# An attention and gated feed-forward kernel whose leftover rows are multiplied as block products of seven

## The chip, the core and the metric

The kernel runs on one core of a Trainium2 chip. The metric is the device time in microseconds (us), the median of several runs. Before the change it is 236.12 us (three runs, 235.85 to 236.62). The profiled execution spans 234.5 us from its first instruction to its last.

## What is computed

There are 8 batches of 8 heads with 576 tokens and 64 features each, and 32 memory slots. The heads of a token (8 x 64 = 512 features) go into a feed-forward block of width 1536.

```python
def _attn_ref(q, k, v, phi):
    a = exp(phi - phi.max(axis=2))         # axis 2: the tokens
    a = a / a.sum(axis=2)
    k_m = np.einsum('bhsm,bhsd->bhmd', a, k)
    v_m = np.einsum('bhsm,bhsd->bhmd', a, v)
    scores = (1 / sqrt(64)) * q @ k_m.T
    return softmax(scores) @ v_m

def _moe_ref(x, w_gate, w_val, w_out):
    g = x @ w_gate
    return silu(g) * (x @ w_val) @ w_out   # x: 4608 tokens x 512
```

(Cut, with softmax and silu written as names.)

## The kernel before

Batches 0 and 1 run together at the start. From batch 2 on, a batch has two parts. In the first, TensorE computes the attention scores, and between them the output products of the batch before. In the second, 24 slots of gate and value products run (`g`), each followed by a silu on ScalarE and a multiplication on VectorE; beside them the sums of the next batch's keys and values (`kv_items`) and the products of its values with the weights (rounds of u: `u_item`, `u_three`) are made, and copied from PSUM by ScalarE and VectorE.

The output product of a batch's first 512 tokens is a 2x2 block product made with seven products of half size instead of eight (`products`). Its sums of blocks, `t_S`, are made by `chunk_done` when a third of the hidden features is ready. Its seven results are combined in three PSUM banks, "homes" `s`, `a` and `c`:

```python
def products(b, by_hand):
    ...
    first = product("s", A(0, 0), W_(0, lo), "p1") + product("a", A(1, 0), W_(1, lo), "c11")
    five = product("c", Sx(0), T(0), "p5")
    six = product("s", Sx(1), T(1), "q6")
    three = product("c", Sx(3), W_(1, hi), "c12")
    seven = product("s", Sx(2), T(2), "c22")
    four = product("s", A(1, 1), T(3), "c21")
    if b + 1 == B:
        return first + six + five + seven + three + four, ops
    return first + five + six + three + seven + four, ops
```

Each `product` has six units of two matmuls with 256 columns. The last 64 tokens of each batch are left over. Two batches' leftovers make 128 rows (`xs[pair]`), which are multiplied plainly, in two column halves:

```python
def out_rest(pair, half):
    ...
    for jf in (2 * n, 2 * n + 1):          # unit n of 6
        nc.tensor.matmul(mine["p"], lhsT=xs[pair][:, jf]..., rhs=WO[jf][:, cols], ...)
    ...                                    # after the last unit: copy, and two stores
```

The main loop takes units from a backlog between other work. What a batch does in its first part, and which units go where:

```python
for b in range(2, B):
    last = b + 1 == B
    exp_tables()
    if b == 2:
        ...
        backlog = one[6:12] + zero[36:] + one[12:36]
        ops = ops1
    else:
        backlog += out_rest(b // 2 - 1, b % 2)
        run(take(6))
    if b > 2:
        loads(b)                           # the loads of batch b + 2
    for g in range(NG):
        scores(b, g)
    ...
    z_inv_v(b, 0)
    norm(b, 0)
    ops["c11"]()
    run(take(6))
    if not last:
        phi_exp(b + 1)
    z_inv_v(b, 1)
    norm(b, 1)
    run(take(6))
    run_late()
    nc.scalar.preload_act_table_set("silu_and_others")
    run(take(12))
    if b == 2:
        u_three(2)
        run(out_rest(0, 0))
        u_values(2)
        backlog = one[36:]
    g = gv_slots(b)
    beside = 0 if last else min(7, len(backlog))
    outs = [lambda: run(take(1)) for _ in range(len(backlog) - beside)]
    streams = [(g, 0, 24), (outs, 4, 24)]
    ...
    if not last:
        load_qT(b + 1)                     # queries transposed by a DMA of SyncE's queue
        if b > 2:
            phi_sum(b + 1)                 # GpSimd sums the phi weights, for kv_denominators
        else:
            streams += [([lambda: loads(2)], 7, 8)]
        streams += [
            (kv_items(b + 1, lambda: (u_item(b, 2, "aava")(), run(take(2)))), KV, KV + 4),
            ([lambda: (run(take(2)), u_three(b + 1), run(take(3)))], 19, 20),
        ]
    spread(*streams)
    flush_mul()
    units, ops = products(b, ("p1", "c11"))
    backlog += units
```

Numbers beside a stream are the slots between which its items are spread. The sums for the next batch begin with its denominators: nine narrow matmuls, or two where GpSimd has summed the weights before (`esums`):

```python
def run_sums():
    ...
    kv_denominators(b, p[0][:, o:o + NG])
    kv_sum(b, p, (0, 1))
    kv_reciprocal(b, p[0][:, o:o + NG])
    kv_norm(b, p)
    done(*p)
    if beside:
        beside()
```

At the end stand the last batch's products, and both halves of the last pair's leftovers; stores then alternate between the queues of SyncE and ScalarE.

Of the kernel before, what the change touches and what calls it, by code (L numbers as in the profile page):

```python
# [14 lines left out]
def kernel(  # L15
# [193 lines left out]
    def phi_sum(b):  # L209

        e = ephis[b].rearrange("p j i m -> p j (i m)")
        mark = att.tile([1, 1], BF16, tag="mark", bufs=1, name="t_mark")
        nc.gpsimd.tensor_copy(out=mark, in_=atts[b - 1, 1][0:1, 0, 0:1])  # L215
        t = att.tile([128, 4, 128], FP32, tag="es", bufs=1, name="t_es")
        add = lambda o, x, y: nc.gpsimd.tensor_tensor(out=o, in0=x, in1=y, op=ALU.add)  # L217
        add(t, e[:, 0:4], e[:, 4:8])
        add(t[:, 0:2], t[:, 0:2], t[:, 2:4])
        add(t[:, 0], t[:, 0], t[:, 1])  # L220
        add(t[:, 0], t[:, 0], e[:, 8])
        hl = att.tile([128, 2, 128], BF16, tag="ehl", bufs=1, name="t_ehl")
        nc.gpsimd.tensor_copy(out=hl[:, 0], in_=t[:, 0])
        nc.gpsimd.tensor_tensor(out=hl[:, 1], in0=t[:, 0], in1=hl[:, 0], op=ALU.subtract)
        esums[b] = hl
# [71 lines left out]
    def kv_items(b, beside=None):  # L297


        def run_sums():  # L300
            o = 2 * D
            p = [bank([128, CH], FP32, f"p_kv{g}") for g in range(NG)]
            kv_denominators(b, p[0][:, o:o + NG])
            kv_sum(b, p, (0, 1))
            kv_reciprocal(b, p[0][:, o:o + NG])
            kv_norm(b, p)
            done(*p)
            if beside:
                beside()

        return [run_sums, lambda: kv_T(b)]
# [273 lines left out]
    def chunk_done(b, c):  # L585
# [21 lines left out]
        end = c + 1 == NCH  # L607
        if (b, c) in ((0, 2), (1, 1), (1, 2)):
            late.append(lambda *part: sums(nc.gpsimd if b else nc.vector, *part))
        else:  # L610
            sums(nc.vector if end else nc.gpsimd)
        if end and b > 1:
            late.append(ends)
        else:
            ends()
        if (b, c) in beside_sums:
            beside_sums[b, c]()

# [4 lines left out]
    }  # L623

# [10 lines left out]
    def store(t_o, b, t0, count, row=0, cols=slice(0, 512), queues=None):  # L635

        if queues is None and box.get("end"):
            queues = nc.sync, nc.scalar
        for n, (r0, m, bb, jj, pp) in enumerate(token_segments(b, t0, count)):
            eng = queues[n % len(queues)] if queues else nc.sync  # L640
            eng.dma_start(out=out_r[bb, jj, pp:pp + m, cols], in_=t_o[row + r0:row + r0 + m])

    def out_rest(pair, half):

        h = DM // 2
        mine = {}
        cols = slice(h * half, h * half + h)

        def unit(n):
            def run():  # L650
                if n == 0:
                    mine["p"] = bank([128, h], FP32, "p_oo")
                for jf in (2 * n, 2 * n + 1):
                    nc.tensor.matmul(  # L654
                        mine["p"],
                        lhsT=xs[pair][:, jf].rearrange("p a t -> p (a t)"),
                        rhs=WO[jf][:, cols],
                        start=(jf == 0),
                        stop=(jf == NJF - 1),
                    )  # L660
                if n == NJF // 2 - 1:
                    t_o = work.tile([128, h], FP32, tag="to", name="t_o")
                    copy("v" if box.get("end") else "a", t_o, mine["p"])
                    done(mine["p"])
                    end = 2 * pair + 2 == B
                    for k in range(2):
                        store(
                            t_o, 2 * pair + k, S - 64, 64, 64 * k, cols,
                            ((nc.sync, nc.scalar)[k],) if end else None,
                        )  # L670

            return run

        return [unit(n) for n in range(NJF // 2)]

    def products(b, by_hand):
# [3 lines left out]
        lo, hi = slice(0, h), slice(h, DM)  # L680

        def A(e, n):
            return lambda c, m, u: hts[b, c][
                :, 2 * m + e, 256 * n + 128 * u:256 * n + 128 * u + 128
            ]

        def Sx(n):
            return lambda c, m, u: Ss[b, c][:, n, m, 128 * u:128 * u + 128]
# [7 lines left out]
        def product(home, lhs, rhs, after):  # L696
            def unit(k):
                c, m = k // 2, k % 2

                def run():  # L700
                    fresh = k == 0 and home not in mine
                    if fresh:
                        mine[home] = bank([128, 2, h], FP32, f"p_o{home}")
                        mine[home, "new"] = True
                    for u in range(2):
# [21 lines left out]
        def keep(name, home):  # L727
            def run():
                nc.scalar.copy(out=tile_of(name, tag=name, bufs=1), in_=mine[home])

            return run
# [6 lines left out]
        def both(name, t0, cols):  # L738
            for u in range(2):
                store(mine[name][:, u, cols], b, t0 + 128 * u, 128, cols=cols)  # L740

        def c11():
            t = tile_of("o1", (128, 2, DM), tag="to")
            add(t[:, :, lo], "a", "p1", True)
            if box.get("end"):
                both("o1", 0, lo)

        def c22():
            t = tile_of("o2", (128, 2, DM), tag="to")
            add(t[:, :, hi], "s", "p5")  # L750
            if box.get("end"):
                both("o2", 256, hi)

        def c12():
            t = mine["o1"]
            add(t[:, :, hi], "c", "q6", True)
            both("o1", 0, hi if box.get("end") else slice(0, DM))

        def c21():
            t = mine["o2"]  # L760
            copy("v" if box.get("end") else "a", t[:, :, lo], mine["s"])
            done(mine["s"])
            both("o2", 256, lo if box.get("end") else slice(0, DM))
# [4 lines left out]
        )  # L768
        now = {n: f for n, f in ops.items() if n not in by_hand}
# [6 lines left out]
        if b + 1 == B:  # L776
# [163 lines left out]
    def loads(b):  # L940

        if b + 2 < B:
            load_q(b + 2)
            load_phi(b + 2, nc.gpsimd)
            load_k(b + 2)
            load_v(b + 2)
# [7 lines left out]
    for b in range(2, B):  # L954
        last = b + 1 == B
        exp_tables()
        if b == 2:
            phi_exp(2)
# [14 lines left out]
            mark = att.tile([1, 1], BF16, tag="mark", bufs=1, name="t_mark")  # L973
            nc.gpsimd.tensor_copy(out=mark, in_=Ts[2][0:1, 3, 0, 0:1])
            for part in ((0, 1), (3,), (2,)):
                for c in (1, 2):
                    sums[1, c](part)
            backlog = one[6:12] + zero[36:] + one[12:36]
            ops = ops1
        else:  # L980
            backlog += out_rest(b // 2 - 1, b % 2)
            run(take(6))
        if b > 2:
            loads(b)
# [9 lines left out]
        norm(b, 0)  # L994
# [5 lines left out]
        norm(b, 1)  # L1000
        run(take(6))
        run_late()
        nc.scalar.preload_act_table_set("silu_and_others")
        run(take(12))
        if b == 2:
            u_three(2)
            run(out_rest(0, 0))
            u_values(2)
            backlog = one[36:]
        g = gv_slots(b)  # L1010
        beside = 0 if last else min(7, len(backlog))
        outs = [lambda: run(take(1)) for _ in range(len(backlog) - beside)]
        streams = [(g, 0, 24), (outs, 4, 24)]
        if last:
            streams += [([u_item(b, 2)], 5, 6)]
        if not last:
            load_qT(b + 1)
            if b > 2:
                phi_sum(b + 1)
            else:  # L1020
                streams += [([lambda: loads(2)], 7, 8)]
            streams += [
                (kv_items(b + 1, lambda: (u_item(b, 2, "aava")(), run(take(2)))), KV, KV + 4),
                ([lambda: (run(take(2)), u_three(b + 1), run(take(3)))], 19, 20),
# [8 lines left out]
    run(out_rest(B // 2 - 1, 0))  # L1033
    box["end"] = True
    run(take(6))
    ops["c11"]()
    run(backlog)
    run(out_rest(B // 2 - 1, 1))
# [28 lines left out]
```

The softmax here doesn't subtract the row's maximum and nothing guards it: scores larger than these inputs give would overflow.

## Time and profile before

| | before |
|---|---|
| median time | 236.12 us |
| span of the profiled execution | 234.5 us |
| TensorE busy | 225.9 us, 96% |
| VectorE busy | 187.4 us, 80% |
| ScalarE busy | 172.5 us, 74% |
| GpSimd busy | 135.2 us, 58% |
| granted TensorE clock | 1.000 |

In the profile, PE is TensorE, PEld its weight loads, DVE VectorE, ACT ScalarE, POOL GpSimd and SP SyncE; a "q" after a name is that engine's queue of transfers. "L706" is a line of the program: in the kernel before, L514 holds the gate and value products, L706 the main output products, L654 the leftovers' products, L471 the rounds of u, L235 and L263 the sums and denominators, L641 the stores. A busy share is time inside records of an instruction; matmul records overlap, so spacing between starts tells more of TensorE than the length of a record. The chain that ended last is followed back from the last instruction to what released it, step by step, and it shows which engine carried the time.

### The profile page before, as it was taken

The page shows a single profiled execution, that of the slowest core. Times are in us where ns is not written, and L with a number is a line of the kernel's source. Part 1 is how long each engine was busy: PE and PEld are TensorE (multiplying, and loading weights), DVE is VectorE, ACT ScalarE, POOL GpSimd, SP SyncE. Part 2 cuts the span into 40 slices and gives each one's busy share as a digit, 9 for nine tenths or more (in the row PEclk, how much of TensorE's full clock was granted, in tenths as well). Part 3 has the DMA queues.
Part 4 walks back from the last instruction along what each step waited for, and adds up shares of the span by engine and source line. Part 5 has one row for each costly group of instructions (what it writes and reads, how often), then busy time and mean ns, then how long its engine had stood idle before and what let it go on. Part 6 is the DMA issues. An engine that isn't in the chain of part 4 may idle for free.

```text
span 234.5 us, 7300 instructions
## 1 busy us (share of the span) xinstructions
PE 225.9 (96%) x2847; PEld 171.3 (73%) x2847; DVE 187.4 (80%) x417; ACT 172.5 (74%) x368; POOL 135.2 (58%) x171
## 2 busy tenths in 40 slices
PE   7998899999999999999999999999999999999992
PEld 2555466778887777887778777877788777878881
DVE  4157699999979697998799878988799879987621
ACT  2758888988447888977898779968897789677310
POOL 8532426999099159654992399267916493029400
PEclk9999999999999999999999999999999999999999
DMA  6999999999974999899559964999313721122134
GB/s 211 205 205 207 198 208 206 228 238 248 207 169 97 252 216 158 166 247 232 137 80 252 214 110 106 225 226 142 110 25 81 132 89 27 31 62 89 33 92 126
DMA packets 42914, 36.84 MB, mean 157 GB/s; under 512 B 15488, under 2 KB 38528, under 8 KB 42880
## 3 DMA queue, kind: packets, MB, share of 16 engines
q0 software_dynamic: 21440, 22.42, 55.0%
q1 hardware_dynamic: 20176, 12.79, 25.8%
q10 hardware_dynamic: 1264, 1.18, 1.6%
q8 instruction: 22, 0.36, 0.6%
q14 instruction: 12, 0.10, 0.1%
HBM read 42.47 MB, written 9.44 MB: 221 GB/s over the span
## 4 chain that ended last, share of the span: by engine, by line
PE 82%; DMA 8%; POOL 4%; DVE 3%; issue 1%; ACT 0%; DVEq 0%; POOLq 0%
PE p_g L514 20%; PE p_v L514 19%; PE p_os L706 16%; PE p_oc L706 8%; DMA t_kv<-in_v_dram 8%; PE p_u L471 5%; PE p_oo L654 5%; PE p_oa L706 4%; PE p_kv L235 2%; POOL t_es L217 1%; POOL t_q L108 1%; PE p_g L400 1%; POOL t_kv L98 1%; DVE t_lz L443 1%; DVE t_z L434 1%
## 5 line engine op out<-in xcount | busy, mean ns | idle before, releaser
L537 DVE TENSOR_TENSOR t_h<-t_sg,p_v 128x288 bf16<-128x288 bf16 x192 | 83.1, 452 | 15.6 <-PE p_v L514 7.6
L514 PEld LDWEIGHTS <-t_U 128*128 128x128 bf16 x768 | 73.7, 98 | 21.7 <-issue 2.9
L531 ACT ACTIVATE t_sg<-p_g 128x288 bf16<-128x288 f32 x192 | 74.5, 423 | 15.9 <-PE p_g L514 9.1
L514 PE MATMUL p_g<-t_A,t_U 128*128 128x288 bf16 x384 | 77.2, 286 | 0.0
L514 PE MATMUL p_v<-t_A,t_U 128*128 128x288 bf16 x384 | 77.0, 286 | 0.0
L706 PEld LDWEIGHTS <-t_S 128*128 128x128 bf16 x384 | 37.4, 98 | 4.5 <-issue 0.2
L601 POOL TENSOR_TENSOR t_S<-t_h 128x512 bf16<-128x512 bf16 x17 | 19.7, 1156 | 35.2 <-DVE t_h L537 35.2
L491 ACT CAST t_U<-p_u 128x512 bf16<-128x512 f32 x53 | 28.0, 608 | 8.9 <-PE p_u L471 8.9
L706 PEld LDWEIGHTS <-t_h 128*128 128x128 bf16 x288 | 27.3, 98 | 7.8 <-issue 4.0
L706 PE MATMUL p_os<-t_T,t_S 128*128 128x256 bf16 x192 | 23.7, 273 | 0.0
L559 POOL TENSOR_TENSOR t_S<-t_S,t_h 128x512 bf16<-128x512 bf16 x17 | 19.6, 1155 | 1.3
L559 POOL TENSOR_TENSOR t_S<-t_h,t_S 128x512 bf16<-128x512 bf16 x17 | 20.1, 1186 | 0.0
L559 POOL TENSOR_TENSOR t_S<-t_h 128x512 bf16<-128x512 bf16 x17 | 19.6, 1155 | 0.0
L471 PE MATMUL p_u<-W,t_kT 64*32 64x512 bf16 (+1 forms) x416 | 15.9, 363 | 0.1
L706 PE MATMUL p_os<-t_T,t_h 128*128 128x256 bf16 x96 | 15.6, 273 | 0.0
L827 PE MATMUL p_warm<-bones 128*128 128x512 bf16 (+2 forms) x43 | 12.9, 427 | 1.7 <-DVE bones L850 1.7
L451 DVE TENSOR_TENSOR t_A<-t_E,t_lz 128x576 bf16<-128x576 bf16 x16 | 13.4, 840 | 0.9 <-ACT t_lz L427 0.3
L654 PE MATMUL p_oo<-WO,t_x 128*128 128x256 bf16 x96 | 14.0, 273 | 0.0
L495 DVE CAST t_U<-p_u 128x512 bf16<-128x512 f32 x19 | 12.4, 683 | 1.6 <-PE p_u L471 1.6
L215 POOL COPY t_mark<-t_A 1x1 bf16<-1x1 bf16 x4 | 0.7, 182 | 20.3 <-DVE t_A L451 20.3
L706 PE MATMUL p_oc<-t_T,t_S 128*128 128x256 bf16 x96 | 12.0, 273 | 0.0
L706 PE MATMUL p_oa<-WO,t_h 128*128 128x256 bf16 x96 | 11.8, 273 | 0.0
(93 smaller groups left out, 309.9 us busy)
## 6 DMA issues: line engine op xcount, KB each, us to landing
t_kv<-in_k_dram POOLq DMA_DIRECT2D x8, 576.0 KB, 10.1
t_kv<-in_v_dram POOLq DMA_DIRECT2D x8, 576.0 KB, 14.4
out_dram<-t_o SPq DMA_DIRECT2D x21, 192.0 KB, 2.6
t_phi<-in_phi_dram POOLq DMA_DIRECT2D x6, 576.0 KB, 7.9
t_q<-in_q_dram POOLq DMA_DIRECT2D x5, 576.0 KB, 7.4
out_dram<-t_o SPq DMA_DIRECT2D x37, 64.0 KB, 2.0
out_dram<-t_o SPq DMA_DIRECT2D x14, 128.0 KB, 5.8
t_q<-in_q_dram POOLq DMA_DIRECT2D x6, 288.0 KB, 11.3
```

The costliest lines, as they stand in the source:

```text
L451: nc.vector.tensor_tensor(out=a, in0=es.pop((b, g)), in1=lzs.pop((b, g)), op=ALU.mult)
L471: nc.tensor.matmul(p[g][32 * i:32 * i + 32, o:o + n], lhsT=kTs[b][64 * g:64 * g + 64, 2, 32 * i:32 * i + 32], rhs=w_part(w, c, i, g, halve ...
L491: nc.scalar.copy(out=t, in_=p)
L495: nc.vector.tensor_copy(out=t, in_=p)
L514: nc.tensor.matmul(p[:, 0:HALF], lhsT=Us[b, c, g][:, o // 2, which, 128 * (o % 2):128 * (o % 2 + 1)], rhs=atts[b, g][:, r], start=(g == 0) ...
L531: nc.scalar.activation(out=sg, in_=gate[:, 0:HALF], func=AF.Silu)
L537: nc.vector.tensor_tensor(out=dst, in0=sg, in1=val[:, 0:HALF], op=ALU.mult)
L559: eng.tensor_tensor(out=out, in0=x, in1=y, op=ALU.subtract)
L601: eng.tensor_tensor(out=t[:, 0], in0=A21, in1=A22, op=ALU.add)
L654: nc.tensor.matmul(mine["p"], lhsT=xs[pair][:, jf].rearrange("p a t -> p (a t)"), rhs=WO[jf][:, cols], start=(jf == 0), stop=(jf == NJF - 1),)
L706: nc.tensor.matmul(mine[home][:, u], lhsT=lhs(c, m, u), rhs=rhs(c, m), start=fresh and u == 0, stop=(k == 5), skip_group_check=u == 1 or n ...
L827: nc.tensor.matmul(p[:, 0:128 * a], lhsT=bones, rhs=x.to_broadcast([128, a, 128]) if a > 1 else bones, start=True, stop=True,)
```

## The change

Four things are changed together.

1. Leftovers of four batches (256 rows, two pairs) are multiplied as one 2x2 block product with seven half-size products: one group in batch 4, one begun in batch 7 and finished at the end. GpSimd makes the four sums of blocks for each third of the hidden features (`quad_sums`). The plain products of leftovers go away.
2. The queries of batch 3 are transposed at the start of batch 2, and loads are issued at the end of a batch's second chunk, for the batch after the next but one.
3. GpSimd's work is set apart from VectorE's: two of the four sums of the second chunk wait until VectorE has done its sums of the third, norms are moved later, the phi weights' sums for batch 5 are left to TensorE, and where they are made, TensorE runs the big sums before the denominators.
4. At the end, the last batch's main stores all go through SyncE's queue, the last three leftover blocks' through two.

The core of the diff (cut where marked):

```diff
         def run_sums():
-            kv_denominators(b, p[0][:, o:o + NG])
+            behind = b in esums
+            if not behind:
+                kv_denominators(b, p[0][:, o:o + NG])
             kv_sum(b, p, (0, 1))
+            if behind:
+                beside()
+                kv_denominators(b, p[0][:, o:o + NG])
             kv_reciprocal(b, p[0][:, o:o + NG])
             kv_norm(b, p)
             done(*p)
-            if beside:
+            if beside and not behind:
                 beside()
...
+        fourth = b in (3, 7)
         if (b, c) in ((0, 2), (1, 1), (1, 2)):
             late.append(...)
+        elif b < 2:
+            sums(nc.gpsimd)
+        elif end:
+            sums(nc.vector)
+            if b + 1 == B:
+                second.pop()(nc.vector, (2, 3))
+                wait_for(Ss[b, 1][0:1, 3, 0, 0:1])
+            else:
+                wait_for(t[0:1, 3, 0, 0:1])
+                second.pop()(nc.gpsimd, (3, 2))
         else:
-            sums(nc.vector if end else nc.gpsimd)
-        if end and b > 1:
+            if c:
+                sums(nc.gpsimd, (0, 1))
+                second.append(sums)
+            else:
+                sums(nc.gpsimd)
+        if end and b > 1 and not fourth:
             late.append(ends)
         else:
             ends()
+        if b > 1 and c == 1:
+            loads(b + 3)
+        if b + 1 == B and end:
+            quad_sums(1)
...
+    def quad_sums(qd):          # x, y = the two pairs; A11, A12 of x, A21, A22 of y
+        for n in range(4):
+            for c in range(NCH):
+                if n == 0:
+                    nc.gpsimd.tensor_tensor(out=t[:, 0], in0=A21, in1=A22, op=ALU.add)
+                elif n == 1:
+                    subtract(nc.gpsimd, t[:, 1], t[:, 0], A11)
+                elif n == 2:
+                    subtract(nc.gpsimd, A21, A11, A21)
+                else:
+                    subtract(nc.gpsimd, t[:, 2], A12, t[:, 1])
...
-        if queues is None and box.get("end"):
-            queues = nc.sync, nc.scalar
-        for n, (r0, m, bb, jj, pp) in enumerate(token_segments(b, t0, count)):
-            eng = queues[n % len(queues)] if queues else nc.sync
+        for r0, m, bb, jj, pp in token_segments(b, t0, count):
+            eng = nc.sync
+            if queues:
+                turn[0] += 1
+                eng = queues[turn[0] % len(queues)]
...
-    def out_rest(pair, half):
-        ...
-    def products(b, by_hand):
+    def products(b, by_hand, quad=None):
+        U = 2 if quad is None else 1        # matmuls in a unit
...
+        def leftover(name, room, half, cols):
+            queues = (nc.sync, nc.scalar) if end and room else None
+            ...                             # add or copy out of PSUM, then two stores
...
         if b == 2:
+            load_qT(3)
...
-            backlog += out_rest(b // 2 - 1, b % 2)
             run(take(6))
-        if b > 2:
-            loads(b)
...
         z_inv_v(b, 0)
-        norm(b, 0)
...
         z_inv_v(b, 1)
-        norm(b, 1)
+        if b > 2:
+            norm(b, 0)
+            norm(b, 1)
         run(take(6))
         run_late()
+        if b == 4:
+            wait_for(atts[4, 1][0:1, 0, 0:1])
+            quad_sums(0)
-        run(take(12))
+        run(take(6))
         if b == 2:
+            norm(2, 0)
+        run(take(6))
+        if b == 2:
+            norm(2, 1)
             u_three(2)
-            run(out_rest(0, 0))
+            run(one[36:39])
             u_values(2)
-            backlog = one[36:]
+            backlog = one[39:]
         g = gv_slots(b)
+        quad = []
+        if b == 4:
+            quad = products(b, (), 0)[0]
+        if last:
+            rest, rest_ops = products(b, (), 1)
+            backlog += rest[:12]
-        beside = 0 if last else min(7, len(backlog))
+        beside = 0 if last else 2 if quad else min(4, len(backlog))
-        streams = [(g, 0, 24), (outs, 4, 24)]
+        streams = [(g, 0, 24), (quad[:12], 0, 3), (quad[12:], 12, 18.5)]
+        streams += [(outs, 4, 7 if quad else 24)]
...
-            load_qT(b + 1)
             if b > 2:
+                load_qT(b + 1)
+            if b > 2 and b != 4:
                 phi_sum(b + 1)
-            else:
-                streams += [([lambda: loads(2)], 7, 8)]
...
-                ([lambda: (run(take(2)), u_three(b + 1), run(take(3)))], 19, 20),
+                ([lambda: (u_three(b + 1), run(take(2)))], 19, 20),
...
-    run(out_rest(B // 2 - 1, 0))
-    box["end"] = True
     run(take(6))
     ops["c11"]()
-    run(backlog)
-    run(out_rest(B // 2 - 1, 1))
+    run(backlog + rest[12:])
```

## The prediction

> **What bounds the kernel now.** I read the page's totals first, then the chain that ended last, then TensorE's waits, then single stretches of the timeline. Totals and chain:
>
> ```profile
> PE 225.9 (96%) x2847; PEld 171.3 (73%) x2847; DVE 187.4 (80%) x417; ACT 172.5 (74%) x368; POOL 135.2 (58%) x171
> ...
> PE 82%; DMA 8%; POOL 4%; DVE 3%; issue 1%; ACT 0%; DVEq 0%; POOLq 0%
> ```
>
> TensorE carries 82% of the chain. The 8% of DMA is the first load, up to about 25 us, which the change doesn't touch. A busy share alone proves little, so I looked at spacing: twelve 256-column products must follow each other without holes if TensorE is the bound. The timeline of TensorE at the end (start, duration, engine, line, operation, tiles, count):
>
> ```profile
> 226.06 1.47 PE L706 MATMUL p_oc<-WO,t_S 128*128 128x256 bf16 x12
> 227.37 1.47 PE L706 MATMUL p_os<-t_T,t_h 128*128 128x256 bf16 x12
> 228.68 1.47 PE L654 MATMUL p_oo<-WO,t_x 128*128 128x256 bf16 x12
> ```
>
> Starts are 1.31 us apart for 12, so **one 256-column product costs 0.109 us**, not the 273 ns of the groups table, whose spans overlap. From the same view a 288-column product costs 0.122. Between 26 and 230 us I find hardly a hole: about 0.18 us at 101.69 (the matmul needs a normalised tile), about 0.2 us near 92.4, and four short ones where batch sums wait for GpSimd:
>
> ```profile
> 105.77 0.47 PE L263 MATMUL p_kv<-ones,t_ehl 128*128 128x2 bf16 x2
> 106.17 0.80 PE L235 MATMUL p_kv<-t_kv,t_ephi 64*32 64x128 bf16 x72
> ```
>
> Two narrow products take 0.40 us from start to the next start. In batch 2, nine of them take 0.30 (58.70 to 59.00), so two should take 0.07: a wait of 0.33. So time falls only if TensorE gets less work or these waits go.
>
> **What the Trainium skill says.** "TensorE: Matmul & The Clock Gate", section "Back-to-back issue gap": spacing of weight-load and matmul pairs, not the length of one record, sets throughput. The trace agrees (0.109 against 273 ns). "SBUF — State Buffer", section "Who interferes with whom": a VectorE instruction with two SBUF inputs contends with a GpSimd instruction that reads SBUF, and one blocks. The trace agrees in batch 2, where a norm takes 1.29 and 1.42 us beside GpSimd's sums and 0.76 us later. "DMA: Bandwidth & Descriptors", section "Issuing engines are not separate DMA queues": issuing from several engines saves only issue time. Here it is that issue time that matters.
>
> **The change, part by part.**
>
> *Products.* Before, the last 64 tokens of two batches form 128 rows: 4 pairs x 2 column halves x 12 = 96 products (line L654). After, two pairs form a 2x2 block product: 2 groups x 7 products x 6 contraction steps = 84. Saved: 12 x 0.109 = **-1.31 us**, all on the bound. By batch, batches 2, 3, 5, 6 each lose 12 products (-1.31 each), batch 4 goes from 12 to 42 (+3.28), batch 7 stays at 12, the end goes from 24 to 30 (+0.66): -1.31 again.
>
> *Sums of the phi weights.* Where GpSimd made them, TensorE now runs the big sums, a round of u and two fillers before it needs them, 1.6 us later. The waits in batches 3, 5, 6 should vanish: 0.33 as above, then 0.26 - 0.07 = 0.19 (156.45 to 156.71) and 0.25 - 0.07 = 0.18 (181.76 to 182.01), so -0.70. Batch 4 no longer makes them for batch 5: nine narrow products (0.30) instead of two with a short wait (131.22 to 131.41, 0.19): +0.11. Together **-0.59**.
>
> *Batch 2's norms* move behind two products, clear of GpSimd's sums. VectorE gets cheaper, but its queue ends later:
>
> ```profile
> 74.58 0.68 DVE L734 TENSOR_TENSOR t_o<-p_oc,t_q 128x512 f32<-128x512 f32 x1
> 75.19 0.68 DVE L734 TENSOR_TENSOR t_o<-p_os,t_p 128x512 f32<-128x512 f32 x1
> 75.78 1.27 DVE L495 CAST t_U<-p_u 128x512 bf16<-128x512 f32 x2
> ```
>
> After, the second addition can't start before its product ends (74.9), then comes the norm (0.76), then the copies from 76.3; the first copy, which the gate products need, ends at 76.95. TensorE, with 6 units of leftovers replaced by 3, would be ready at 76.6. So about 0.4 of its saving is lost: **+0.40**.
>
> *Early transpose.* The transposed queries of batch 3 were issued at 79.03 and landed 15.0 us later, at 94.0, with first use at 94.55. A shorter batch 2 alone would run into that. Issued at about 60 it is out of the way. The loads too are issued earlier, at the end of the second chunk, so they collide less with the transposes (3.0 us of issue without loads beside it, 9.3 with). This protects the gain, it doesn't make any: 0.
>
> *Less filler.* VectorE is busy 13.5 of 16.2 us in such a stretch (127.49 to 143.68), ScalarE 12.9. Six leftover units (1.31 us) were part of what TensorE ran there, and now it waits sooner for banks. In batch 4 the small product holds a second bank while the sums' banks wait 1.2 us for VectorE. At the end each small product lasts only 0.66 us, about as long as the copy (0.42) plus two hand-offs that frees its bank. I guess 0.3 for batch 4, 0.3 over batches 3, 5, 6, 0.15 at the end, and enter half, since many such waits never come: **+0.35**.
>
> *Last stores.* Batch 7's main stores alternated between two queues, now all go through SyncE's. One queue takes 1.75 us for four:
>
> ```profile
> 190.05 1.75 SPq L641 DMA_DIRECT2D out_dram<-t_o  x4
> ```
>
> Count from E, the end of batch 7's product "seven" (226.06 before). Its stores start at E+0.98 (227.04 in the trace), the next group may start at E+2.29 and the third at E+3.54. On one queue: 0.98 to 2.75, then 2.8 to 4.75 (four of the other shape take 1.95), then 4.8 to 6.55. The small products end at E+5.90; the copy of the very last is done 0.66 later, at E+6.56. But SyncE still owes three leftover stores, 0.51 each: the last is issued at about E+7.6. **+1.05**. What speaks for the new scheme: ScalarE no longer stands behind store issues when its copies free a bank.
>
> Sum: -1.31 - 0.59 + 0.40 + 0.35 + 1.05 = **-0.10**, so 236.0 from 236.12.
>
> **Rivals.** (1) *The tail is free*: the one queue isn't late, or the final two queues absorb it. Then about -1.15: 235.0. For it: stores land in about 2 us. Against it: three 4-store groups arrive every 1.3 us and take about 1.8. (2) *ScalarE and VectorE become the bound* in the gate-value stretches of batches 2, 3, 5, 6. For it: six copies come in one burst. Against it: those engines are idle 2.7 us or more in each stretch. If half of each 1.31 were lost, +2.0 on rival 1: 237.0. (3) *A transfer or GpSimd becomes late*: batch 4 gives GpSimd twelve more sums, 7 us at half of 1.16 us each, before its own chunk sums. Then a product waits several us: 238 or more. Against it: its first results are needed only at slot 12, some 8 us later, and the phi sums it used to make there (3.9 us, 152.69 to 156.55 in the batch shown by the same view) are gone. (4) *All hidden waits go too*, the two holes at 92.4 and 101.7 included: 234.5.
>
> **Range and chances.** The only certain term is -1.31. Taking the tail away gives 235.0, taking the guessed waits away as well 234.6; doubling the waits I fear gives 237.5. So **236.0, range 234.6 to 237.5**. Faster by over 2% would need 231.4, below what all terms together offer: 0.02. Slower by over 2% needs 240.8, a serious new wait: 0.03. Within 2%: 0.95.
>
> **What would show it.** Step 1: 84 leftover products instead of 96 at 0.109 spacing. Step 2: two narrow products directly after the fillers, without a hole. Step 3: a hole of about 0.4 us before the first gate product of batch 2. Step 4: starts of batch 3's scores without a wait for a transpose. Step 5: small holes around the rounds of u and in batch 4. Step 6: SyncE's queue unbroken over the last 6 us, its last store issued about 1 us after the last copy. The prediction is wrong if the queue is free when the last copy ends (too slow), or if TensorE waits in batch 4 for GpSimd's twelve sums (too fast).

## The result, and the profile after

| | before | after |
|---|---|---|
| median time, 6 runs each | 236.11 us | 237.76 us |
| ratio to before, 95% interval | | 1.0061 (1.0043 to 1.0079) |
| span of the profiled execution | 234.5 us | 236.0 us |
| start of the last matmul | 229.88 us | 229.89 us |
| start of the last store | 230.65 us | 232.72 us |

The change made the kernel slower by 0.6%. (The ratio is not the quotient of the two medians, which is 1.0070.) The measured 237.76 us lies above the predicted range, which ended at 237.5, and "236.0" had the wrong direction. In the kernel after, L518 holds the gate and value products, L739 all output products, leftovers included, L475 the rounds of u, L234 and L262 the sums and denominators, L699 the stores. Its totals and chain, from the page:

```profile
PE 225.2 (95%) x2842; PEld 170.2 (72%) x2842; DVE 184.8 (78%) x425; ACT 173.0 (73%) x368; POOL 143.9 (61%) x193
...
PE 84%; DMA 9%; POOL 2%; DVE 1%; issue 1%; ACT 0%; POOLq 0%
```

TensorE is still the bound. But it ends where it ended before, although it has less work. Its end in the timeline (start, duration, engine, line, operation, tiles, count):

```profile
225.33 1.47 PE L739 MATMUL p_os<-t_T,t_h 128*128 128x256 bf16 x12
226.64 0.82 PE L739 MATMUL p_os<-t_T,t_Q 128*128 128x256 bf16 x6
...
229.35 0.81 PE L739 MATMUL p_os<-t_T,t_x 128*128 128x256 bf16 x6
```

The small products follow each other at 0.66 us for six, the same 0.109 us per product. So the products cost what was counted. Behind them, VectorE's last copy and SyncE's queue in the kernel after:

```profile
230.20 0.42 DVE L337 COPY t_q<-p_os 128x256 f32<-128x256 f32 x1 [0.29 <-PE p_os L739]
```

```profile
228.93 2.38 SPq L699 DMA_DIRECT2D out_dram<-t_o  x4
231.41 0.57 SPq L699 DMA_DIRECT2D out_dram<-t_p  x1
232.07 1.18 SPq L699 DMA_DIRECT2D out_dram<-t_q  x2
```

The last data is ready at 230.62, and the queue is then still at the main stores; the last of its seven stores starts at 232.72, 2.1 us late. The same in the kernel before, where the last store started 0.04 us after its copy (it is the second of the two in the queue's line):

```profile
230.19 0.42 DVE L333 COPY t_o<-p_oo 128x256 f32<-128x256 f32 x1 [0.62 <-PE p_oo L654]
```

```profile
229.97 1.15 SPq L641 DMA_DIRECT2D out_dram<-t_o  x2
```

From the starts of the score products, batch by batch (in us; "predicted" are the prediction's terms for that batch, without the 0.35 that it spread over all):

| from scores to scores | before | after | change | predicted |
|---|---|---|---|---|
| batch 2 | 30.78 | 30.07 | -0.71 | -0.91 |
| batch 3 | 25.63 | 24.45 | -1.18 | -1.64 |
| batch 4 | 25.24 | 29.01 | +3.77 | +3.39 |
| batch 5 | 25.30 | 24.03 | -1.27 | -1.50 |
| batch 6 | 25.30 | 24.03 | -1.27 | -1.49 |
| batch 7, to the last matmul | 33.87 | 34.61 | +0.74 | +0.66 |

Batches 2, 3, 5 and 6 win, but each wins too little. Four places in the profile after show where. A "hole" below is what a step from start to start takes beyond the usual spacing of such products. First, the denominators in batch 3:

```profile
104.34 0.41 PE L518 MATMUL p_v<-t_A,t_U 128*128 128x288 bf16 x2
104.68 0.80 PE L234 MATMUL p_kv<-t_kv,t_ephi 64*32 64x128 bf16 x72
...
105.86 0.61 PE L739 MATMUL p_os<-t_T,t_h 128*128 128x256 bf16 x4
106.31 0.19 PE L262 MATMUL p_kv<-ones,t_ehl 128*128 128x2 bf16 x2
106.36 0.41 PE L518 MATMUL p_g<-t_A,t_U 128*128 128x288 bf16 x2
```

Two narrow products now take 0.05 us to the next start, where it was 0.40: no wait is left. But the 0.40 also held the step into the sums, and that step now stands ahead of the sums: from 104.34 to 104.68 it is 0.34 us, where two products of this kind take 0.245, so 0.09 are spent there. The gain is 0.26, not 0.35. Second, the round of u in batch 3, in the chain in order of time (start, duration, what):

```profile
109.45 3.69 DMA t_kT<-t_bkv
113.14 0.04 issue
113.19 0.84 PE p_u L475 x24
```

TensorE had a hole of 0.52 us for want of the transposed sums, which a transfer of SyncE's queue brings; where nothing is missing, a step into a round of u takes 0.09. Third, batch 2's first gate product, with VectorE's and then TensorE's timeline:

```profile
75.42 0.75 DVE L455 TENSOR_TENSOR t_A<-t_E,t_lz 128x576 bf16<-128x576 bf16 x1
76.09 1.28 DVE L499 CAST t_U<-p_u 128x512 bf16<-128x512 f32 x2
```

```profile
76.30 0.41 PE L475 MATMUL p_u<-W,t_kT 64*32 64x512 bf16 x8
76.82 0.65 PE L518 MATMUL p_g<-t_A,t_U 128*128 128x288 bf16 x4
```

The gate product waits for the first of VectorE's two copies, as predicted. From the last start of u to its own it is 0.49 us; before the change it was 0.31, which a step from u to gate products takes anyway. Together with 0.11 us more ahead of the three units, 0.29 us are lost here. Fourth, the end of batch 5's stretch, ScalarE's timeline, then VectorE's and TensorE's:

```profile
166.70 2.05 ACT L495 CAST t_U<-p_u 128x512 bf16<-128x512 f32 x4 [0.20 <-PE p_u L475]
168.61 0.63 ACT L335 COPY t_o<-p_os 128x512 f32<-128x512 f32 x1
169.09 1.38 ACT L535 ACTIVATE t_sg<-p_g 128x288 bf16<-128x288 f32 x4
```

```profile
169.59 1.18 DVE L541 TENSOR_TENSOR t_h<-t_sg,p_v 128x288 bf16<-128x288 bf16 x3 [0.93 <-ACT t_sg L535]
```

```profile
168.92 0.41 PE L518 MATMUL p_g<-t_A,t_U 128*128 128x288 bf16 x2
169.29 0.72 PE L518 MATMUL p_v<-t_A,t_U 128*128 128x288 bf16 x4
```

ScalarE copies for 2.5 us without a silu between, VectorE waits 0.93 us for a silu, and TensorE shows holes of 0.13 and 0.07 us (that a bank isn't free is inferred). The same two holes stand in batches 3 and 6. In the kernel before, batches 3 to 6 have none there; batch 5's last gate and value products:

```profile
168.58 0.41 PE L514 MATMUL p_g<-t_A,t_U 128*128 128x288 bf16 x2
168.82 0.65 PE L514 MATMUL p_v<-t_A,t_U 128*128 128x288 bf16 x4
```

### The profile page after: what moved, and what is told of

It is laid out like the page before. It is cut to its first block, busy times and chain, and to the rows that moved or that the text cites. A ratio compares the mean times of both kernels' runs of the same rounds, so it can differ in the third digit from the quotient of the medians.

```text
span 236.0 us, 7323 instructions
## 1 busy us (share of the span) xinstructions
PE 225.2 (95%) x2842; PEld 170.2 (72%) x2842; DVE 184.8 (78%) x425; ACT 173.0 (73%) x368; POOL 143.9 (61%) x193
## 4 chain that ended last, share of the span: by engine, by line
PE 84%; DMA 9%; POOL 2%; DVE 1%; issue 1%; ACT 0%; POOLq 0%
PE p_os L739 20%; PE p_g L518 20%; PE p_v L518 20%; PE p_oc L739 10%; DMA t_kv<-in_v_dram 8%; PE p_oa L739 5%; PE p_u L475 5%; PE p_kv L234 2%; DMA t_kT<-t_bkv 2%; POOL t_q L108 1%; PE p_g L404 1%; POOL t_kv L98 1%; PE p_q L381 0%; DVE t_bkv L270 0%; POOL t_kv L102 0%
## 5 line engine op out<-in xcount | busy, mean ns | idle before, releaser
L541 DVE TENSOR_TENSOR t_h<-t_sg,p_v 128x288 bf16<-128x288 bf16 x192 | 81.9, 452 | 17.6 <-PE p_v L518 7.1
L518 PEld LDWEIGHTS <-t_U 128*128 128x128 bf16 x768 | 73.8, 98 | 22.6 <-issue 3.4
L518 PE MATMUL p_g<-t_A,t_U 128*128 128x288 bf16 x384 | 77.2, 286 | 0.2
L518 PE MATMUL p_v<-t_A,t_U 128*128 128x288 bf16 x384 | 77.2, 286 | 0.1
L739 PEld LDWEIGHTS <-t_S 128*128 128x128 bf16 x384 | 37.4, 98 | 4.6 <-issue 0.2
L605 POOL TENSOR_TENSOR t_S<-t_h 128x512 bf16<-128x512 bf16 x17 | 19.6, 1154 | 31.4 <-DVE t_h L541 31.4
L739 PEld LDWEIGHTS <-t_h 128*128 128x128 bf16 x288 | 26.9, 98 | 9.3 <-issue 5.8
L739 PE MATMUL p_os<-t_T,t_S 128*128 128x256 bf16 x192 | 23.7, 273 | 0.0
L563 POOL TENSOR_TENSOR t_S<-t_h 128x512 bf16<-128x512 bf16 x16 | 18.4, 1153 | 0.0
L563 POOL TENSOR_TENSOR t_S<-t_h,t_S 128x512 bf16<-128x512 bf16 x16 | 18.4, 1152 | 0.0
L475 PE MATMUL p_u<-W,t_kT 64*32 64x512 bf16 (+1 forms) x416 | 15.9, 363 | 0.4 <-DMA t_kT<-t_bkv 0.4
L739 PE MATMUL p_os<-t_T,t_h 128*128 128x256 bf16 x96 | 15.2, 274 | 0.0
L739 PE MATMUL p_oc<-t_T,t_S 128*128 128x256 bf16 x96 | 12.0, 273 | 0.0
L739 PE MATMUL p_oa<-WO,t_h 128*128 128x256 bf16 x96 | 11.8, 273 | 0.0
L739 PE MATMUL p_oc<-WO,t_S 128*128 128x256 bf16 x96 | 11.8, 272 | 0.0
L739 PE MATMUL p_os<-WO,t_h 128*128 128x256 bf16 x96 | 11.8, 272 | 0.0
L455 DVE TENSOR_TENSOR t_A<-t_E,t_lz 128x576 bf16<-128x576 bf16 x16 | 11.4, 740 | 0.3 <-ACT t_lz L431 0.3
```

The lines of the kernel that those rows point to most:

```text
L455: nc.vector.tensor_tensor(out=a, in0=es.pop((b, g)), in1=lzs.pop((b, g)), op=ALU.mult)
L475: nc.tensor.matmul(p[g][32 * i:32 * i + 32, o:o + n], lhsT=kTs[b][64 * g:64 * g + 64, 2, 32 * i:32 * i + 32], rhs=w_part(w, c, i, g, halve ...
L518: nc.tensor.matmul(p[:, 0:HALF], lhsT=Us[b, c, g][:, o // 2, which, 128 * (o % 2):128 * (o % 2 + 1)], rhs=atts[b, g][:, r], start=(g == 0) ...
L541: nc.vector.tensor_tensor(out=dst, in0=sg, in1=val[:, 0:HALF], op=ALU.mult)
L563: eng.tensor_tensor(out=out, in0=x, in1=y, op=ALU.subtract)
L605: eng.tensor_tensor(out=t[:, 0], in0=A21, in1=A22, op=ALU.add)
```

## The experiments

Ratios are to the kernel before, run beside each kernel on the same chip. Its median there was 236.48 us for the first four experiments (44 runs, 235.84 to 237.74), 236.94 for the next four (30 runs, 235.94 to 237.99) and 236.37 for the last two (11 runs, 235.97 to 237.57), so medians of different groups aren't to be set against each other. The kernel after wasn't run again beside them: what separates a run from it is read from the profiles, one execution each. Times of single events are from these profiles too.

**Main stores on two queues again** (undoes the first half of part 4 alone).

```diff
-        for r0, m, bb, jj, pp in token_segments(b, t0, count):
+        for n, (r0, m, bb, jj, pp) in enumerate(token_segments(b, t0, count)):
             eng = nc.sync
+            if queues is None and box.get("end"):      # set before the last main products
+                eng = (nc.sync, nc.scalar)[n % 2]
```

> The changed kernel with the last batch's main stores again alternating between SyncE's and ScalarE's queues. Theory A (SyncE's queue is the tail): the last store, issued 2.8 us after the last matmul in the changed kernel, comes back to within 1 us of it, and the time falls by about 1.0 us net. Theory B (ScalarE then stands behind its store issues, its copies out of PSUM come late, TensorE waits): TensorE's last matmul comes 0.5 to 0.9 us later, so that the net is nearer to 0.5 us. Theory C (only lost TensorE time made the change slower, the tail is hidden by landing): no difference beyond 0.2 us.

Measured: 237.93 us, ratio 1.0051 (1.0038 to 1.0065). The last store starts 0.94 us after the last matmul instead of 2.83, so the queue is mended. But the last matmul comes 1.3 us later, in spite of a batch 3 that was 0.3 us shorter in this run. TensorE's waits, and ScalarE's timeline:

```profile
PE p_os L741 <- ACT t_q L766: 1.3, 2, 0.9
```

```profile
225.67 3.07 ACTq L701 DMA_DIRECT2D out_dram<-t_o  x5
228.84 0.37 ACT L766 COPY t_q<-p_os 128x256 f32<-128x256 f32 x1 [5.44 <-DMA out_dram<-t_o]
229.23 0.37 ACT L766 COPY t_p<-p_oc 128x256 f32<-128x256 f32 x1
```

Both A and B hold, and cancel: ScalarE's copy that frees bank `s` stands behind its store issues until 228.84, and TensorE waits 0.9 us for it. The delay of 1.3 us is larger than B's. The single queue of the change was a real answer to a real wait, at the same price.

**Transpose of batch 4's sums by TensorE.**

```diff
-        if b > 3:
+        if b > 4:
             nc.sync.dma_start_transpose(out=kTs[b], ...)
```

> The changed kernel with the transposed key and value sums of batch 4 made by TensorE and copied by VectorE, as batches 2 and 3 do it, instead of by a transfer of SyncE's queue. Theory A (the 0.52 us that TensorE stands before the round of u in batch 3 is the wait for that transfer): the hole goes, three transposes (about 0.17 us) come, net 0.3 us faster. Theory B (it is the PSUM banks or ScalarE that hold the round up, the transfer only ends at about the same time): the hole stays at 0.3 us or more, and the time gets 0.1 to 0.2 us longer.

Measured: 237.97 us, ratio 1.0057 (1.0040 to 1.0075). The hole before the round of u is the usual 0.09 us, so the 0.52 was the transfer's. But nothing is gained: a hole of 0.25 us appears before the three transposes, which now wait for VectorE's scaled sums, and the transposes take 0.18. The hole itself also varies: with the same code it was 0.52, 0.19 and 0.16 us in the profiles of after, of the first experiment and of the next.

**Batch 2's norms back in their old place.**

```diff
         z_inv_v(b, 0)
+        if b == 2:
+            norm(2, 0)
         ops["c11"]()
...
-        if b > 2:
-            norm(b, 0)
-            norm(b, 1)
+        if b > 2:
+            norm(b, 0)
+        norm(b, 1)
```

> The changed kernel with batch 2's two norms back where they were, each straight after its sums, beside GpSimd's sums. Theory A (VectorE's queue was made later by moving them, so the first gate product waits): the hole of 0.49 us before the first gate product of batch 2 shrinks by about 0.4 us, the norms take 1.3 to 1.4 us again, and the time falls by 0.3 to 0.4 us. Theory B (the move was right, the contention with GpSimd costs more than it saves): the gate products of batch 2 start later than in the changed kernel, and the time is the same or up to 0.5 us longer.

Measured: 237.81 us, ratio 1.0057 (1.0034 to 1.0079). The norms took 1.28 and 1.42 us again, the gate products began at 76.95 instead of 76.82, and the stretch ended at the same time (92.27 and 92.24). TensorE's timeline shows what took the wait's place:

```profile
74.71 0.84 PE L475 MATMUL p_u<-W,t_kT 64*32 64x512 bf16 x24
75.87 0.81 PE L739 MATMUL p_os<-t_T,t_h 128*128 128x256 bf16 x6 [0.32 <-DVE t_o L769]
```

The three units of the product "four" now wait for VectorE's addition on their bank. So the order of the norms only moves the wait in batch 2. What both orders share is that the 12 plain leftover products are gone that lay there and needed nothing from VectorE. That this is the cause is the reading that fits; no run put them back.

**All filler units ahead of the big round of u.** (Filler units are those of the main products that are still in the backlog; the expectation calls them leftover units.)

```diff
-        beside = 0 if last else 2 if quad else min(4, len(backlog))
+        beside = 0 if last else 2
...
-        streams += [(outs, 4, 7 if quad else 24)]
+        streams += [(outs, 4, 7 if quad else 24 if last else 19)]
```

> The changed kernel with the leftover units of batches 3, 5 and 6 (and 2) all before the big round of u, none after it. Theory A (ScalarE's 512-column copy of the last main block stands right behind the four copies of the round of u, and so delays the silus): that copy moves to the middle of the stretch, the holes of 0.13 and 0.07 us at the end of each stretch shrink, and 0.1 to 0.2 us come back in each of three batches, 0.3 to 0.6 us in all. Theory B (with few fillers left TensorE runs into its banks after the round of u whatever the order, and more so with none after it): new holes of 0.2 us or more after the round, and the time is the same or up to 0.6 us longer.

Measured: 236.97 us, ratio 1.0011 (0.9995 to 1.0027). The last matmul is 0.78 us earlier than in after. Of this 0.27 comes in batch 2, 0.46 in batch 3, 0.04 each in batches 5 and 6. About half is what A said. In batch 2 the copy no longer stands ahead of the last silus; ScalarE's timeline in after and in this run:

```profile
91.12 0.63 ACT L335 COPY t_o<-p_os 128x512 f32<-128x512 f32 x1
91.60 1.38 ACT L535 ACTIVATE t_sg<-p_g 128x288 bf16<-128x288 f32 x4
```

```profile
91.37 1.36 ACT L535 ACTIVATE t_sg<-p_g 128x288 bf16<-128x288 f32 x4
```

TensorE's holes of 0.10, 0.25 and 0.07 us at the end of that stretch become 0.08 and 0.07, and in batches 3, 5 and 6 the hole of 0.13 becomes 0.08. The other half is the transfer in batch 3: the hole there is the usual 0.09. The queries' transpose held the queue for 4.03 us instead of 5.95, and the sums' transpose was issued at 107.79 instead of 109.45 and landed 2.0 us before the round of u. Why the first of them was shorter isn't shown; four stores that began at 91.78, beside the loads, began at 85.78 here. As that hole was only 0.16 and 0.19 in other profiles without this edit, its size in one profile is partly chance. No larger holes come after the round, against B.

**Denominators first.**

```diff
-            behind = b in esums
+            behind = False
```

> The changed kernel with the denominators of the next batch again before the big sums, the round of u and the fillers. Theory A (the prediction's step: the reordering takes away TensorE's wait for GpSimd's sums of the phi weights): waits of 0.2 to 0.5 us in front of the sums come back in batches 3, 5 and 6, TensorE's last matmul comes about 0.7 us later. Theory B (GpSimd would be in time in the changed kernel anyway, the reordering gives nothing, or takes banks for longer): no more than 0.2 us either way.

Measured: 238.69 us, ratio 1.0086 (1.0064 to 1.0107); last matmul 0.88 us later. In TensorE's timeline of batch 5 the wait is back:

```profile
158.12 0.17 PE L262 MATMUL p_kv<-ones,t_ehl 128*128 128x2 bf16 x1
158.50 0.18 PE L262 MATMUL p_kv<-ones,t_ehl 128*128 128x2 bf16 x1 [0.22 <-POOL t_ehl L223]
```

It costs 0.40 us in each of batches 5 and 6. In batch 3 it costs nothing: TensorE waits for GpSimd and then finds the transfer landed (hole 0.12 instead of 0.52). A held. In the changed kernel the step saves more than it does against the kernel before, since the wait would be longer here: 0.38 us between the two narrow products of batch 5, where it was 0.15.

**One queue in the kernel before.**

```diff
-            queues = nc.sync, nc.scalar
+            queues = nc.sync,
```

> The kernel before, in which only the last batch's main stores go through SyncE's queue alone instead of alternating with ScalarE's. Theory A (twelve store issues in a row at 0.45 to 0.5 us each make a queue that outlives the products): SyncE's last store is issued about 2 us later than before, 2.8 us after the last matmul, and the time grows by 1.4 to 2 us. Theory B (the long tail of the changed kernel belongs to its six extra small stores and ScalarE's issues beside them, not to the main stores): the time grows by 0.5 us or less.

Measured: 238.35 us, ratio 1.0090 (1.0058 to 1.0122). The last matmul is where it was (229.73), the last store starts at 232.92. SyncE's timeline over the end:

```profile
228.72 4.67 SPq L641 DMA_DIRECT2D out_dram<-t_o  x9
```

Nine stores, 4.67 us, with hardly a hole. A held; the last store is even 3.2 us behind the last matmul. This edit alone, with none of the change's products, makes the kernel about as slow as the whole change.

**A mixed tail.** Two of the three late groups of main stores alternate, and only the last, which would stand before ScalarE's copies, stays on SyncE's queue.

```diff
-        def both(name, t0, cols):
+        def both(name, t0, cols, two=False):
             for u in range(U):
-                store(mine[name][:, u, cols], b, t0 + 128 * u, 128, cols=cols)
+                queues = (nc.sync, nc.scalar) if two else None
+                store(mine[name][:, u, cols], b, t0 + 128 * u, 128, cols=cols, queues=queues)
...
-                both("o2", 256, hi)
+                both("o2", 256, hi, True)
...
-            both("o1", 0, hi if end else slice(0, DM))
+            both("o1", 0, hi if end else slice(0, DM), end)
```

> The changed kernel with two of the three late groups of main stores (blocks 22 and 12) alternating between both queues, and only the last group (block 21) on SyncE's alone. Theory A (one queue is too slow for all, and ScalarE's stores hurt only where they stand before its two copies for the small products, which is the last group): TensorE's last matmul stays where it is in the changed kernel (within 0.3 us), the last store is issued within 1.1 us of it instead of 2.8, and the time falls by 0.8 to 1.5 us. Theory B (any store on ScalarE delays its copies): TensorE ends 0.4 us or more later and the gain is under 0.8 us.

Measured: 236.0 us, ratio 0.9966 (0.9955 to 0.9976): faster than the kernel before beside it (236.94), with all else as in the change; the profiled spans, 234.4 and 234.5 us, are level. A held. SyncE's timeline:

```profile
224.90 4.30 SPq L699 DMA_DIRECT2D out_dram<-t_o  x8
229.30 0.47 SPq L699 DMA_DIRECT2D out_dram<-t_p  x1
229.87 1.44 SPq L699 DMA_DIRECT2D out_dram<-t_q  x2
```

Eight main stores instead of twelve, and the three small ones follow their data. The last matmul is at 229.81 (229.89 after), so no copy is late; the last store starts at 230.91, 1.10 us behind it. From the last matmul to the end of the span it is 4.6 us instead of 6.1.

**All mends together:** the mixed tail, the filler units ahead, and two smaller ones.

```diff
-            behind = b in esums
+            behind = b > 3
...
         z_inv_v(b, 1)
+        norm(b, 0)
         if b > 2:
-            norm(b, 0)
             norm(b, 1)
...                                        # batch 2's second norm one product earlier
```

> The changed kernel with the mixed tail, all leftover units before the big round of u, the denominators after the sums for batch 5 too, and batch 2's first norm straight after the softmax sums while its second comes ahead of the product that ends last. Theory A (the loss of the change is these waits: tail about 1.2, the transfer and the filler order 0.8, batch 2's gate wait up to 0.5, batch 4's bank wait 0.3): 234.9 to 235.6 us, faster than the kernel before. Theory B (each mended wait uncovers another right behind it, ScalarE and VectorE being nearly full): 236 us or more.

Measured: 235.59 us, ratio 0.9956 (0.9941 to 0.9972). A as to direction, but only at the edge of its range, and about as much as the tail and the order of the filler units give: the last matmul comes 0.64 us earlier than in after. The mends of batches 2 and 4 gave next to nothing: the gate products of batch 2 began 0.1 to 0.2 us earlier, and batch 4's bank wait of 0.29 us turned into holes of 0.08 and 0.24.

**Loads late.** The loads alone are put back to a batch's start.

```diff
-        if b > 1 and c == 1:
-            loads(b + 3)
...
+        if b > 2:
+            loads(b + 2)
         for g in range(NG):
             scores(b, g)
```

> The changed kernel with the loads of the batch after the next issued at the start of a batch, as before the change, instead of at the end of the second chunk of the batch before; the early transpose of batch 3's queries stays. Theory A (the prediction's step: earlier loads collide less with the transposes): the transpose of queries in batch 3 takes longer than the 5.95 us of the changed kernel, the sums' transpose behind it lands later, and TensorE's wait before the round of u in batch 3 grows by 0.3 us or more. Theory B (the transposes meet the same loads either way): issue times of the transposes within 0.5 us of the changed kernel, the time the same within 0.3 us.

Measured: 254.12 us, ratio 1.074 (1.0706 to 1.0774). Here batch 5's loads are issued from 97.79 on, behind two of GpSimd's sums that the change had moved there, so 3 us later than in the kernel before (94.64). This isn't the old timing, then: the run shows what late loads cost, not what the earlier ones of the change save. TensorE's waits, SyncE's timeline, and a table of three stretches (start and end; length; busy time and count of PE, PEld, DVE, ACT and POOL; clock; DMA):

```profile
PE p_u L475 <- DMA t_kT<-t_bkv: 11.8, 3, 5.3
```

```profile
103.61 8.30 SPq L121 DMA_TRANSPOSE t_qT<-t_q  x1
112.02 2.66 SPq L288 DMA_TRANSPOSE t_kT<-t_bkv  x1
```

```profile
106.00:112.60 6.60, 6.60 (x65) 5.37 (x58) 6.21 (x17) 5.76 (x14) 4.19 (x4) 1.00 1.20 223
117.50:122.40 4.90, 4.81 (x40) 2.58 (x41) 2.17 (x4) 3.27 (x7) 0.00 (x0) 0.51 0.09 24
125.00:131.00 6.00, 6.00 (x69) 5.17 (x54) 5.84 (x12) 5.69 (x11) 5.18 (x8) 1.00 0.11 7
```

The queries' transpose takes 8.30 us of the queue instead of 5.95, the sums' transpose behind it is issued 2.6 us later and lands 5.5 us after that. TensorE stands for 4.8 us in batch 3. Then its clock is 0.51 for some 5 us: two products of a gate start 0.48 us from the next two, where it is 0.245. Three waits, 11.8 us together, and the slower clock behind the long ones make the 15 us of span.

**All mends, and one copy moved from ScalarE to VectorE** in each big round of u from batch 3 on.

```diff
-        u_round(b, (((0,), 0, (0, 1)), ((1,), 0, (0, 1)), ((0,), 1, (0, 1))), "avaava")
+        u_round(b, (((0,), 0, (0, 1)), ((1,), 0, (0, 1)), ((0,), 1, (0, 1))),
+                "avaava" if b == 2 else "avavav")
```

> The kernel with all mends, in which the big round of u from batch 3 on gives three of its six copies to VectorE instead of two (ScalarE three instead of four). Theory A (ScalarE's burst of four copies delays the silus, which is what holds TensorE's banks at the end of a stretch): the holes of 0.08 and 0.07 us at the end of the stretches of batches 3 to 6 go, 0.1 us each, 0.4 us in all. Theory B (VectorE, the busier of the two, then delays its multiplications): the holes grow, and the time is the same or up to 0.4 us longer.

Measured: 234.69 us, ratio 0.9918 (0.9897 to 0.9940), the fastest kernel of this study. The two holes at the end of each stretch are gone in batches 2 to 6, 0.15 us each, so A holds, with 0.7 us in all instead of 0.4. The last matmul starts at 228.51, 1.4 us before that of the kernel before. That kernel wasn't run with the copy moved; in its trace only batch 2 has such holes (0.13 and 0.07), so little would be won there. Its page:

```profile
span 232.8 us, 7326 instructions
...
PE 224.4 (96%) x2842; PEld 170.0 (73%) x2842; DVE 187.1 (80%) x430; ACT 170.3 (73%) x363; POOL 144.4 (62%) x193
```

## Why the prediction was wrong, step by step

Two terms carry most of the miss. "Less filler" was entered at +0.35 and measured about +1.0, and "Last stores" was entered at +1.05 and cost +1.43. In both the mechanism was named rightly and the size was too small. A transfer that was entered at 0 cost 0.43, and the sums of the phi weights gave 0.36 instead of 0.59.

**What bounds the kernel**: right. TensorE's starts fix the time up to the last matmul: the fourth and fifth experiments moved it by -0.78 and +0.88 us, and the span by -0.8 and +0.8.

**Products, -1.31**: right in size (12 products fewer at 0.109 us). The saving was spent again.

**Sums of the phi weights, -0.59**: the waits went, but the gain was counted too large. The prediction scaled nine narrow products at 0.30 us down to two at 0.07. But narrow products start 0.025 us apart, 0.09 of the 0.30 is the step into the sums, and in the kernel after that step still takes 0.09. Measured with that step on both sides, the four batches give -0.26, -0.11, -0.10 and +0.11, together -0.36.

**Batch 2's norms, +0.40**: measured 0.29, so the size was about right, but the order of the norms isn't what makes the wait. The third experiment has a loss of the same size with the norms in their old place.

**Early transpose and loads, 0**: failed in batch 3. The step saw that they protect the gain, and the ninth experiment shows what is at stake: over 15 us with loads 3 us later than before the change. It missed that the protection isn't complete: the queries' transpose in batch 3 still held the queue for 5.95 us (6.00 before), the sums' transpose queues behind it, and the round of u, moved forward by the missing fillers, came 0.43 us too soon in the profile of after (0.07 to 0.10 in those of the first and third experiments). The trace of before had the number: issued at 110.76, with 3.6 us or more to land, the sums were there at most 0.55 us before the round at 114.91.

**Less filler, +0.35**: this step is the one that failed by most. It listed 0.3 for batch 4, 0.3 over batches 3, 5 and 6 and 0.15 at the end, and entered half. What TensorE lost beyond the named terms is a remainder: the changes in the table of batches add up to +0.08, and -1.31 - 0.36 + 0.29 + 0.43 gives -0.95, so 1.0 us is left. By batch it is 0.31 in batch 2, which the step hadn't listed, 0.38 in batch 4, 0.15 and 0.14 in batches 5 and 6, 0.08 at the end, and nothing in batch 3, where the hole of 0.18 that the kernel before had at 101.7 is gone. Holes of about these sizes stand in the trace: in batch 2 those of 0.10, 0.25 and 0.07 where before there were 0.13 and 0.07, and two of 0.07 and 0.06 behind the first gate products; in batch 4 one of 0.29 behind the fillers, and 0.08 and 0.07 at the end; in batches 5 and 6 the 0.13 and 0.07. The fourth and the last experiment take most of those at the ends away by moving ScalarE's copies. For the 0.29 the trace names VectorE's scaling of the sums (`t_bkv`), whose bank the next gate product seems to wait for, as the step had feared; no run tests that alone.

**Last stores, +1.05**: the mechanism was right, the size wrong. Counted from the end of "seven", the twelve main stores end at E+7.3 (predicted 6.55), and the last small one starts at E+8.7 (7.6). A small store takes 0.66 us from start to start, not 0.51: its issue took 0.54 to 0.57 us, and 0.1 lies between two, where a separate instruction waits for semaphores. And main stores rose from 0.42 to 0.6 or 0.7 us where ScalarE issued its own beside them (that the one causes the other wasn't tested). The start of the last store moved by 2.07 us. The rest of the program behind it was 0.63 us shorter than before (3.24 against 3.87), so 1.4 us reached the span. What the step left out was the choice between the queues: its last sentence names ScalarE's copies, and of the two experiments on it the first shows that two queues for all cost as much, the seventh that a mix has less of both costs.

So the sum reads: 0.01 at TensorE instead of -1.15, +2.06 instead of +1.05 at the stores, -0.63 behind them: +1.44 of span. Rival 2, ScalarE and VectorE near their limit, was partly right; rival 3 was right about a transfer and wrong about GpSimd, whose twelve sums were in time. Neither of the two signs that the prediction named for being wrong came: the queue was not free when the last copy ended, and TensorE did not wait for GpSimd in batch 4.

## What to carry to other kernels

Here, work that was taken off the bound engine had also been a pause for its neighbours. Before counting a saving in full, look at each wait that ended just before the removed piece, and at what would now be needed earlier. Count a queue's stores at the end of a kernel one by one, from when their data is ready, and give a second queue only those that don't stand before a copy on which products wait. A guess of waits that is read from the trace engine by engine shouldn't be halved on a feeling: here even the whole guess, 0.75 us, fell short of 1.0. And when a short piece of work is moved or scaled, take the step into the next kind of work out of its time first.

## What the runs showed of the hardware

In the ninth experiment a wait of 4.8 us took TensorE's clock to half for the next 5 us (0.51 in the stretch above). A wait of 5.5 us did the same (0.50 from 180 to 183 us), and after one of 2.1 us the clock stayed at 1.00 (151.1 to 153.0). Batch 3 took 30.75 us instead of 24.45; 4.25 of the 6.30 are the longer wait, and the other 2 come with the slower clock. The Trainium skill, "TensorE: Matmul & The Clock Gate", section "What's actually happening", gives an idle window of about 3.4 us as what throttles the array, and these three waits agree with it. And a store issue of at most 96 rows, 0.32 to 0.69 us of a queue from 225 us on in the kernel after, isn't small where a dozen or more of them stand in one queue at the end: the one-queue edit alone cost 0.9% of the time (0.6 to 1.2).
